# Both mix weights loaded and copied on GpSimd's queue, values loaded two per period, and transfers of the later stages regrouped, in a fused attention, MLP and top-1 mixture kernel

## The chip, the cores and the metric

The kernel runs on one NeuronCore of a Trainium2 chip. The metric is the device time of one execution in microseconds; the time before is the median of three runs. Besides these there is one profiled execution, with a trace of every instruction.

## The reference

Three stages follow each other on 1792 tokens (4 batches of 448) of width 768 (12 heads of 64). Everything is fp32.

```python
def _attn_ref(q, k, v, w_pre, w_post):
    scores = scale * np.matmul(q, k.transpose(0, 1, 3, 2))
    scores = np.einsum('bhij,hg->bgij', scores, w_pre)      # 12x12 mix of the heads
    attn = softmax(scores)                                   # over the keys
    attn = np.einsum('bhij,hg->bgij', attn, w_post)          # 12x12 mix again
    return np.matmul(attn, v)
...
def _moe_ref(x, w_in, w_out):                                # 768 -> 2048 -> 768
    h = x @ w_in
    g = np.where(h > 0.0, h, np.exp(np.minimum(h, 0.0)) - 1.0)
    return g @ w_out
...
def _moe2_ref(x, w_skip, w_gate, w1, w2):                    # 8 experts, 768 -> 1024 -> 768
    do_compute = x @ w_skip > 0
    logits = x @ w_gate
    e_idx, gate_w = argmax(logits), max(softmax(logits))
    y = gate_w * (relu(x @ w1[e_idx]) @ w2[e_idx])           # row by row
    return where(do_compute, x + y, x)
...
    x = _attn_ref(q, k, v, w_pre, w_post).transpose(0, 2, 1, 3).reshape(1792, 768)
    return _moe2_ref(_moe_ref(x, ...), ...)
```

## The kernel before

**Precision.** TensorE multiplies in fp32r. Most operands are split into a high part (a cast on ScalarE) and a low part (a subtraction on VectorE), and each product is made of three matmuls: high by high, low by high, high by low. So each loaded tile passes through two engines before TensorE can use it.

**Attention.** q is handled in tiles of at most 120 queries, k in six pairs of heads per batch. `qk` makes scores and writes them to `s`. `relayout` copies `s` by DMAs on SyncE's queue to tiles `d` (eight, whose first 32 rows are zeroed once by GpSimd memsets, L185), in which queries and heads share the partitions, so that the 12x12 mix becomes a matmul with a matrix that is built once from w_pre (`kpre_low`, `kpre_up`, in `mix_pre`). Softmax follows, then the second mix (`mix_post`, matmul `f`, with `kr`, which is `kposts` scaled by the row sums on GpSimd), then the product with v (`av`). The work runs in periods n: period n mixes units n, ends unit n-1 and computes the scores of a later tile. `load_mix` broadcasts w_pre and w_post, 10 rows of copies each (`pre`, `post`); `kron` spreads each to a block matrix by a VectorE copy and two GpSimd selects; `kposts` then gets three more copies by DMA (L381). All loads and stores of this stage go out on SyncE's queue, in the order of the code. Six values (`v`, one per pair of heads) are loaded at the start of period 0; for the other batches the list `values` is filled as the last tile of a batch is done, two at a time.

**MLP.** Weights come as fp64 bit pieces and are narrowed on the chip to fp32 and partly kept in DRAM (`wf`). `products(s)` makes h (L626), `elu` stores the activations to `gT` in DRAM. `tables()` loads `wgt` (gate and skip weights), turns it by 12 small matmuls, and writes it out as `wg`, which is read back later by a broadcast as `wrow`.

**MLP's second product and routing.** Main loop over 14 token tiles of 128 rows, L899. The last weight pieces are loaded singly by L845 into `raw0`'s two-piece buffers, three in all, split into `w`, and used by tile 0. `load_g(i)` loads tile i's activations `gr` in four pieces. `score` multiplies the finished rows by `wrow` on VectorE; `route` and `seat` give each row a slot with its expert; the two `place_old` calls put rows into the first expert tile while the last are being scored.

**Experts.** `use()` hands out weight parts, each 128x1536, split by ScalarE (`whi`) and VectorE (`wlo`). `gather` fetches an expert's rows `xg` by an indirect DMA from GpSimd's queue; TensorE turns them (`pt`, L1082), and they are split to `xt`. `expert_first` and `expert_second` are an expert's two products. From the fourth expert on the order of experts is decided on the chip: `plan()` computes `swap`, and `reorder()` applies it to the row lists `ids` and gives `ordered`, which the gather of expert 3 and later ones needs.

The order on each engine is the order of the code. What an engine does next waits for semaphores, and nothing behind it on the same engine goes ahead.

Of the kernel before, what the change touches and what calls it, by code (L numbers as in the profile page):

```python
# [8 lines left out]
FP32 = mybir.dt.float32  # L9
# [4 lines left out]
ALU = mybir.AluOpType  # L14
# [64 lines left out]
def attention(tc, q, k, v, w_pre, w_post, xT, mix):  # L79
# [12 lines left out]
    with ExitStack() as ctx, ExitStack() as mixing, ExitStack() as scoring:  # L92
# [90 lines left out]
        n_d = [0]  # L183
        for t in d_all:
            nc.gpsimd.memset(t[:32], 0.0)  # L185

# [129 lines left out]
        def load_mix(w, name):  # L316
            rep = const.tile([BR * H, H], FP32, name=name)
            nc.sync.dma_start(out=rep, in_=w.unsqueeze(0).to_broadcast([BR, H, H]))
            return rep
# [20 lines left out]


        for u in range(3):
            load_q(0, [(2 * u, 2 * u + 2)])
            for p in (2 * u, 2 * u + 1):
                load_k(0, p)
                if p >= 4:
                    break
            if u == 0:
                pre, post = load_mix(w_pre, "pre"), load_mix(w_post, "post")
            if u == 2:  # L350
                split_q(0, 0)
                split_k(0, 0, nc.vector)
                load_k(0, 5)
# [3 lines left out]
        for p in range(NK):  # L357
# [8 lines left out]
            if p == 2:  # L366
# [13 lines left out]
                for z, first in ((1, UP), (0, GAP), (0, UP + GAP)):  # L380
                    nc.sync.dma_start(out=kposts[z][first:first + HP, :], in_=kposts[1][:HP, :])  # L381
        moves.pop()()
# [10 lines left out]
        for n in range(NP):  # L393
# [10 lines left out]
            late = n >= NP - 5  # L404
            while values:
                load_v(*values.pop(0))
            if T2 < len(tiles):
# [68 lines left out]
def mixtures(tc, order, xT, w_in, w_out, w_skip, w_gate, w1, w2, ident, gT, wf, wg, x2d, slots, out):  # L476
# [5 lines left out]
    with ExitStack() as top:  # L482
# [27 lines left out]
        with ExitStack() as ctx:  # L510
# [63 lines left out]
            def tables():  # L574
# [7 lines left out]
                nc.sync.dma_start(out=x2d[NT:NT + 1, :], in_=wgs[0:1, :])  # L582
                nc.sync.dma_start(out=wgt[:, :, :E], in_=w_gate.rearrange("(k p) e -> p k e", p=128))
                nc.sync.dma_start(out=wgt[:, :, E], in_=w_skip.rearrange("(k p) -> p k", p=128))
                nc.sync.dma_start(out=wg[E:E + 1, :], in_=w_skip.unsqueeze(0))
# [125 lines left out]
            elu(1)  # L711
            load_x(3)
            products(2)
            w_jobs(0)
# [30 lines left out]
        with ExitStack() as ctx:  # L745
# [47 lines left out]
            def route(i, lg):  # L793
                mx = st_p.tile([128, 8], FP32, tag="mx", name="mx")
                nc.vector.max(out=mx, in_=lg[:, :E])
                ix = st_p.tile([128, 8], U32, tag="ix", name="ix")
                nc.vector.max_index(out=ix, in_max=mx, in_values=lg[:, :E])
                nmx = st_p.tile([128, 1], FP32, tag="nmx", name="nmx")
                nc.vector.tensor_scalar(out=nmx, in0=mx[:, 0:1], scalar1=-1.0, scalar2=None, op0=ALU.mult)
                ex = st_p.tile([128, E], FP32, tag="ex", name="ex")  # L800
                sm = st_p.tile([128, 1], FP32, tag="sm", name="sm")
                nc.scalar.activation(out=ex, in_=lg[:, :E], func=ACTF.Exp, bias=nmx, accum_out=sm)
                nc.vector.tensor_scalar(out=sm, in0=sm, scalar1=1e-9, scalar2=None, op0=ALU.add)
                nc.vector.reciprocal(out=pairs[:, i, 1:2].bitcast(FP32), in_=sm)
                ef = st_p.tile([128, 1], FP32, tag="ef", name="ef")
                nc.vector.tensor_copy(out=ef, in_=ix[:, 0:1])
                do = st_p.tile([128, 1], FP32, tag="do", name="do")
                nc.vector.tensor_scalar(out=do, in0=lg[:, E:E + 1], scalar1=0.0, scalar2=None, op0=ALU.is_gt)
                oh = st_p.tile([128, E], FP32, tag="oh", name="oh")
                nc.vector.tensor_scalar(out=oh, in0=iota8, scalar1=ef, scalar2=do, op0=ALU.is_equal, op1=ALU.mult)  # L810
                return i, oh, do
# [30 lines left out]
            gs = {0: load_g(0)}  # L842
            for fc in range(EARLY, NF):
                raw = raw0.tile([128, 2 * DM], FP32, tag="w", name="wr")[:, :DM]
                last_wr = nc.sync.dma_start(out=raw, in_=wf[fc - EARLY])  # L845
                wo[fc] = split(raw, ring_a if fc < RA + RB else ring2)
            for part in (slice(0, 5), slice(5, E + 1)):
# [40 lines left out]
            for i, n, fc, cs in work:  # L888
# [35 lines left out]
                if fc == NF - 1:  # L924
                    if 0 in cs:
                        x2 = rows[i] = x2_p.tile([128, DM], FP32, tag="x2", name="x2")
                    for c in cs:
                        to, at = x2[:, cols[c]], po[c][:, :cols[c].stop - cols[c].start]
                        nc.scalar.copy(out=to, in_=at)  # L929
                        if last and c == 1:  # L930
                            turned, freed = score_turned(x2, c)
                            place_old(range(2))
                            logits(turned)
                            place_old(range(2, 5))
                    if 1 in cs:
# [3 lines left out]
            hot = seat(*route(NTILE - 1, lg))  # L939
            place_old(range(5, NK))  # L940
            xt0 = [gh_p.tile([128, 2, GC, 128], FP32R, tag="gh", name=f"xt0{c}") for c in range(2)]
# [8 lines left out]
        with ExitStack() as ctx:  # L950
# [288 lines left out]
            h, ht = new_h(), []  # L1239
            expert_first([0], [h], jobs(((3, 2), turn_h, h, ht, 0)))  # L1240
            expert_second(0, ht, jobs(((0,), turn_h, h, ht, 1), ((2,), turn_x, 1)))
            h = new_h()
            expert_first([1], [h], jobs(((1, 2), turn_x, 2)))
            reorder()
            xg[3] = gather(ids[3])
            base = nc.values_load(tab[0:1, 3, E:E + 1], engines=(SP,), min_val=0, max_val=E * CAP)
# [110 lines left out]
```

## Time and profile before

| what | value |
|---|---|
| median of 3 runs | 1022.62 us (1020.44 to 1026.99) |
| profiled execution, its own time | 1024.68 us |
| its span in the trace | 1022.9 us |
| mean granted clock of TensorE | 0.988 |
| TensorE busy | 982.5 us, 96% |
| VectorE, ScalarE, GpSimd busy | 71%, 54%, 22% |

1.8 us of the profiled time lie outside the span. TensorE is busy for all but 40.4 us of the span, so the table says that a reader has to look for the places where TensorE does nothing, and at what it waits for there.

### The profile page before, as it was taken

The numbers are of one execution on the slowest core, as the hardware profiler recorded it, in microseconds if no ns is written. First come the engines' busy times: TensorE is split into PE (matmuls) and PEld (weight loads), VectorE is DVE, ScalarE is ACT, GpSimd is POOL, SyncE is SP. The second block draws the span as 40 slices with busy tenths as digits, with TensorE's granted clock in tenths as the row PEclk, the third lists the DMA queues.
The fourth block names the chain that finished last, engine by engine and source line by source line (L and its number), as shares of the span: only waits on it lengthen the run. The fifth ranks groups of instructions, "written<-read, shape, count | busy, mean of one in ns | idle before, by whom it ended". The sixth has DMA issues, their size and how long they took to land. (4 is left out here: it accounts for less than half of the span.)

```text
span 1022.9 us, 30007 instructions
## 1 busy us (share of the span) xinstructions
PE 982.5 (96%) x12226; PEld 860.5 (84%) x12226; DVE 725.8 (71%) x1458; ACT 555.9 (54%) x1121; POOL 226.8 (22%) x295
## 2 busy tenths in 40 slices
PE   7899999999998899999999999999999999899997
PEld 4577777777766788999999999999999988799987
DVE  5677776777765777666666477777777748999963
ACT  5687787788765654445444462222222116788851
POOL 2233224224223312232332200010101003321002
PEclk9999999999998989999999999999999999999999
DMA  4665665675646565454665489543434396999800
GB/s 157 214 206 158 218 208 149 205 235 131 216 167 204 160 220 166 156 183 151 227 220 192 140 281 301 155 124 93 123 95 123 99 344 237 393 396 398 322 9 34
DMA packets 132297, 199.67 MB, mean 195 GB/s; under 512 B 35476, under 2 KB 99480, under 8 KB 131901
## 3 DMA queue, kind: packets, MB, share of 16 engines
q1 hardware_dynamic: 130013, 191.27, 56.4%
q0 software_dynamic: 2144, 6.46, 1.6%
q8 instruction: 97, 1.59, 0.7%
q14 instruction: 43, 0.35, 0.1%
HBM read 122.47 MB, written 37.65 MB: 157 GB/s over the span
## 5 line engine op out<-in xcount | busy, mean ns | idle before, releaser
L899 PE MATMUL o<-w,gh 128*128 128x384 f32 (+2 forms) x1344 | 239.2, 337 | 1.2 <-DVE w L505 0.8
L899 PEld LDWEIGHTS o<-w,gh 128*128 128x128 f32 x1344 | 231.9, 188 | 4.5 <-DVE w L505 1.4
L626 PE MATMUL h<-xh,w 128*128 128x448 f32 x1152 | 235.4, 367 | 0.0
L626 PEld LDWEIGHTS h<-xh,w 128*128 128x128 f32 x1152 | 217.4, 189 | 17.3 <-issue 0.4
L265 PEld LDWEIGHTS f<-kr,e 64*64 64x64 f32 x5888 | 106.3, 136 | 39.1 <-issue 29.5
L213 DVE TENSOR_REDUCE nmx<-c 128x1 f32<-128x448 f32 x184 | 102.4, 617 | 51.7 <-PE c L205 51.6
L226 ACT ACTIVATE e<-c,nmx 128x448 f32<-128x448 f32 x184 | 114.2, 632 | 23.0 <-DVE nmx L213 22.8
L789 DVE SCALAR_TENSOR_TENSOR junk<-x,wrow 128x768 f32<-128x768 f32 x117 | 111.8, 955 | 18.3 <-ACT x L929 12.8
L246 POOL TENSOR_SCALAR kr<-kpost,rs 128x60 f32<-128x60 f32 x184 | 78.4, 448 | 200.1 <-DVE rs L241 110.2
L1067 DVE TENSOR_TENSOR wlo<-w1t,whi 128x1536 fp32r<-128x1536 f32 x64 | 111.0, 1751 | 14.3 <-ACT whi L1065 14.0
L265 PE MATMUL f<-kr,e 64*64 64x60 f32 (+1 forms) x5888 | 108.4, 219 | 7.3 <-issue 3.5
L541 POOL TENSOR_TENSOR wf<-a,p 128x768 f32<-128x768 f32 x32 | 66.6, 2081 | 187.2 <-DVE p L539 139.5
L1065 ACT CAST whi<-w1t 128x1536 fp32r<-128x1536 f32 x64 | 93.9, 1482 | 20.6 <-PE ph L1094 9.4
L164 PE MATMUL qk<-k,qq 64*120 64x448 f32 (+1 forms) x576 | 82.6, 408 | 8.1 <-ACT k L135 4.5
L774 ACT CAST gh<-gr 128x512 fp32r<-128x512 f32 x56 | 35.0, 624 | 98.7 <-PE o L899 39.1
L205 PE MATMUL c<-d,kpre_low 64*64 64x448 f32 x368 | 83.3, 554 | 3.0 <-ACT s L168 2.8
L205 PE MATMUL c<-d,kpre_up 60*64 60x448 f32 x368 | 81.8, 554 | 0.0
L271 ACT COPY at<-f 128x420 f32<-128x420 f32 (+1 forms) x136 | 65.4, 516 | 28.2 <-PE f L265 27.2
L164 PEld LDWEIGHTS qk<-k,qq 64*120 64x120 f32 (+1 forms) x576 | 52.1, 186 | 27.8 <-issue 4.6
L286 PE MATMUL xp<-at,v 128*64 128x120 f32 (+1 forms) x1152 | 67.5, 266 | 7.3 <-issue 3.9
L168 ACT ACTIVATE s<-qk 120x448 f32<-120x448 f32 (+1 forms) x96 | 51.7, 544 | 35.5 <-PE qk L164 26.4
L169 DVE TENSOR_SCALAR s<-qk 120x448 f32<-120x448 f32 (+1 forms) x96 | 58.3, 621 | 16.1 <-PE qk L164 8.4
(180 smaller groups left out, 1255.7 us busy)
## 6 DMA issues: line engine op xcount, KB each, us to landing
w1t<-in_moe_w_dram SPq DMA_DIRECT2D x64, 768.0 KB
d<-s SPq DMA_DIRECT2D x176, 210.0 KB
gT<-g SPq DMA_DIRECT2D x64, 224.0 KB
f<-in_moe_w_in_dram SPq DMA_DIRECT2D x16, 768.0 KB
f<-in_moe_w_out_dram SPq DMA_DIRECT2D x16, 768.0 KB
gr<-gT SPq DMA_DIRECT2D x48, 256.0 KB
rk<-in_k_dram SPq DMA_DIRECT2D x24, 224.0 KB
v<-in_v_dram SPq DMA_DIRECT2D x24, 224.0 KB
```

What stands on the lines that cost most here:

```text
L164: nc.tensor.matmul(out=ps[:n, :S], lhsT=qt[T, p // 2][rows, a, p % 2, :n], rhs=kt[b, p][rows, z, :], start=(i == 0), stop=(i == 2))
L205: nc.tensor.matmul(out=ps[j * UP:(j + 1) * UP, :S], lhsT=kpre_up[UP:UP + HP, :] if z else kpre_low, rhs=d[z, j])
L213: nc.vector.tensor_reduce(out=t, in_=c, op=ALU.max, axis=AX.X, negate=True)
L226: nc.scalar.activation(out=e, in_=c, func=ACTF.Exp, bias=t, accum_out=sms[0][:, k + i:k + i + 1])
L246: nc.gpsimd.tensor_scalar(out=kr, in0=kposts[z], scalar1=rs[:, 2 * i + z:2 * i + z + 1], scalar2=None, op0=ALU.mult)
L265: nc.tensor.matmul(out=ps[to, heads, z, :], lhsT=e[rows, keys * JW:(keys + 1) * JW], rhs=kr[rows, first * HR:(first + n) * HR])
L286: nc.tensor.matmul(out=ps[i][z * 64:(z + 1) * 64, :n], lhsT=vt[b, p][:, jc * 2 + z, :], rhs=att[T][:, jc * H + ORDER.index(2 * p + z), :n] ...
L626: nc.tensor.matmul(out=ps, lhsT=w[:, a, kk, :], rhs=xs[tb, kk][:, z, :], start=(kk == 0 and a + z == 0), stop=(kk == NK - 1 and a == 1))
L789: nc.vector.scalar_tensor_tensor(out=t[:, o:o + n], in0=x2, scalar=1.0, in1=w, op0=ALU.mult, op1=ALU.mult, accum_out=lg[:, e:e + 1])
L899: mm = nc.tensor.matmul(out=po[c][:, :cols[c].stop - cols[c].start], lhsT=gs[i][fc // GC][:, a, fc % GC, :], rhs=wo[fc][:, z, cols[c]], st ...
L1065: nc.scalar.copy(out=hi, in_=t)
L1067: nc.vector.tensor_tensor(out=lo, in0=t, in1=hi, op=ALU.subtract)
```

## The change

Seven edits stand in the diff. `pre` and `post` are loaded on GpSimd's queue, ahead of the eight memsets of `d`, and the three copies to `kposts` go out there too. Values are loaded from period 1 on, two per period. The two loads of `wgt` move from `tables()` to a place behind `load_x(3)`, ahead of `products(2)`. The last weight pieces of the MLP are loaded two to a buffer, so that six are under way at once instead of three. `route` computes `oh` ahead of the exponential. One of the pieces of `place_old` moves behind the last `route`. `reorder()` and the gather of expert 3 move ahead of the second product of expert 0.

```diff
-        for t in d_all:
-            nc.gpsimd.memset(t[:32], 0.0)
...
         def load_mix(w, name):
             rep = const.tile([BR * H, H], FP32, name=name)
-            nc.sync.dma_start(out=rep, in_=w.unsqueeze(0).to_broadcast([BR, H, H]))
+            nc.gpsimd.dma_start(out=rep, in_=w.unsqueeze(0).to_broadcast([BR, H, H]))
             return rep
...
+        pre, post = load_mix(w_pre, "pre"), load_mix(w_post, "post")
+        for t in d_all:
+            nc.gpsimd.memset(t[:32], 0.0)
         for u in range(3):
             load_q(0, [(2 * u, 2 * u + 2)])
             for p in (2 * u, 2 * u + 1):
                 load_k(0, p)
                 if p >= 4:
                     break
-            if u == 0:
-                pre, post = load_mix(w_pre, "pre"), load_mix(w_post, "post")
...
                 for z, first in ((1, UP), (0, GAP), (0, UP + GAP)):
-                    nc.sync.dma_start(out=kposts[z][first:first + HP, :], in_=kposts[1][:HP, :])
+                    nc.gpsimd.dma_start(out=kposts[z][first:first + HP, :], in_=kposts[1][:HP, :])
...
-            while values:
-                load_v(*values.pop(0))
+            for bp in values[:2] if n else ():
+                load_v(*bp)
+            del values[:2 if n else 0]
...
-                nc.sync.dma_start(out=wgt[:, :, :E], in_=w_gate.rearrange("(k p) e -> p k e", p=128))
-                nc.sync.dma_start(out=wgt[:, :, E], in_=w_skip.rearrange("(k p) -> p k", p=128))
                 nc.sync.dma_start(out=wg[E:E + 1, :], in_=w_skip.unsqueeze(0))
...
             elu(1)
             load_x(3)
+            nc.sync.dma_start(out=wgt[:, :, :E], in_=w_gate.rearrange("(k p) e -> p k e", p=128))
+            nc.sync.dma_start(out=wgt[:, :, E], in_=w_skip.rearrange("(k p) -> p k", p=128))
             products(2)
...
             gs = {0: load_g(0)}
-            for fc in range(EARLY, NF):
-                raw = raw0.tile([128, 2 * DM], FP32, tag="w", name="wr")[:, :DM]
-                last_wr = nc.sync.dma_start(out=raw, in_=wf[fc - EARLY])
-                wo[fc] = split(raw, ring_a if fc < RA + RB else ring2)
+            for f0 in range(EARLY, NF, 2):
+                raw = raw0.tile([128, 2, DM], FP32, tag="w", name="wr")
+                fcs = range(f0, min(f0 + 2, NF))
+                for fc in fcs:
+                    last_wr = nc.sync.dma_start(out=raw[:, fc - f0], in_=wf[fc - EARLY])
+                for fc in fcs:
+                    wo[fc] = split(raw[:, fc - f0], ring_a if fc < RA + RB else ring2)
...
-                            place_old(range(2, 5))
+                            place_old(range(2, 4))
...
             hot = seat(*route(NTILE - 1, lg))
-            place_old(range(5, NK))
+            place_old(range(4, NK))
...
             expert_first([0], [h], jobs(((3, 2), turn_h, h, ht, 0)))
+            reorder()
+            xg[3] = gather(ids[3])
             expert_second(0, ht, jobs(((0,), turn_h, h, ht, 1), ((2,), turn_x, 1)))
             h = new_h()
             expert_first([1], [h], jobs(((1, 2), turn_x, 2)))
-            reorder()
-            xg[3] = gather(ids[3])
```

In `route` the four operations that make `ef`, `do` and `oh` now stand ahead of those that make `nmx`, `ex` and `sm`; each of them is the same as before.

The first place is SyncE's queue at the change from the first score tile to the first period. Each row is a DMA that the engine issues, with the line, the destination, the source and its size; `d_154` to `d_157` are the last four copies of the first score tile. Before:

```order
L197 DMA d_161<-s 120x1x448
L129 DMA v<-in_v_dram 128x448 x6
L197 DMA d_154<-s 120x1x448
L197 DMA d_155<-s 120x1x448
L197 DMA d_156<-s 120x1x448
L197 DMA d_157<-s 120x1x448
L197 DMA d_158<-s 120x1x448
```

And in the changed kernel:

```order
L195 DMA d_161<-s 120x1x448
L195 DMA d_154<-s 120x1x448
L195 DMA d_155<-s 120x1x448
L195 DMA d_156<-s 120x1x448
L195 DMA d_157<-s 120x1x448
L129 DMA v<-in_v_dram 128x448 x2
L195 DMA d_158<-s 120x1x448
```

The six loads of values stood ahead of the four copies; two of them stand behind now, and the other four in the two periods after that.

The second place is SyncE's queue at the start of the MLP's second product: `wr` are the last weight pieces, `gr` activations of the coming tiles, `wrow` the broadcast gate weights. Before:

```order
L845 DMA wr<-wf_79 128x768
L771 DMA gr<-gT_0_61 128x4x128
L771 DMA gr<-gT_0_65 128x4x128
L637 DMA gT_3_76<-g 128x448
L771 DMA gr<-gT_0_69 128x4x128
L845 DMA wr<-wf_80 128x768
L771 DMA gr<-gT_0_73 128x4x128
L771 DMA gr<-gT_0_61 128x4x128
L845 DMA wr<-wf_81 128x768
L845 DMA wr<-wf_82 128x768
L845 DMA wr<-wf_83 128x768
L849 DMA wrow<-wg 128x3840
```

And in the changed kernel:

```order
L847 DMA wr<-wf_79 128x768
L847 DMA wr<-wf_80 128x768
L635 DMA gT_3_76<-g 128x448
L847 DMA wr<-wf_81 128x768
L847 DMA wr<-wf_82 128x768
L771 DMA gr<-gT_0_61 128x4x128
L771 DMA gr<-gT_0_65 128x4x128
L847 DMA wr<-wf_83 128x768
L852 DMA wrow<-wg 128x3840
L852 DMA wrow<-wg 128x3072
L771 DMA gr<-gT_0_69 128x4x128
L771 DMA gr<-gT_0_73 128x4x128
```

The weight pieces stand together and ahead of the activations, and the last two activations of tile 1 stand behind both halves of `wrow`.

The third place is VectorE in the first expert: `wlo` are weight parts, `ht` turned hidden rows, `swapped` the work of `reorder()`, and the small rows are those of `plan()`. Before:

```order
L976 CAST pair<-ix 128x1
L995 TENSOR_SCALAR ni<-ni 1x8
L1067 TENSOR_TENSOR wlo<-w1t,whi 128x1536
L978 TENSOR_SCALAR pbase<-pair 128x1
L997 TENSOR_SCALAR ov<-ni 1x8
L1084 TENSOR_TENSOR ht_12859<-pt_12860,ht_12859 128x512
L980 TENSOR_SCALAR star<-ebase,pbase 128x8
L989 TENSOR_SCALAR tab<-pbase 1x1
L1067 TENSOR_TENSOR wlo<-w1t,whi 128x1536
```

And in the changed kernel:

```order
L979 CAST pair<-ix 128x1
L998 TENSOR_SCALAR ni<-ni 1x8
L1034 TENSOR_TENSOR swapped<-ids 128x8
L981 TENSOR_SCALAR pbase<-pair 128x1
L1000 TENSOR_SCALAR ov<-ni 1x8
L1070 TENSOR_TENSOR wlo<-w1t,whi 128x1536
L983 TENSOR_SCALAR star<-ebase,pbase 128x8
L992 TENSOR_SCALAR tab<-pbase 1x1
L1087 TENSOR_TENSOR ht_12856<-pt_12857,ht_12856 128x512
L984 TENSOR_SCALAR swap<-star 128x8
L988 TENSOR_TENSOR last<-last,star 1x8
L1001 TENSOR_TENSOR ov<-ov,star 1x8
```

The first operation of `reorder()` that reads `ids` now stands ahead of a weight part. The next weight part stood three rows behind the first `ht`; now 13 rows lie between them, four of them operations of `reorder()`, one the second `ht`, the others those of `plan()`.

## Rows read from the trace of the kernel before

**Rows 1.** Waits of TensorE over the whole span: us in total, times, longest.

```profile
PE pt L1082 <- DMA xg<-x2d,ordered: 3.0, 1, 3.0
...
PE c L205 <- ACT s L168: 2.8, 1, 2.8
PE pt L589 <- DMA wgt<-in_moe_w_gate_dram: 2.2, 1, 2.2
...
PE o L899 <- DVE w L505: 0.8, 2, 0.4
...
PE o L899 <- ACT w L504: 0.4, 2, 0.2
```

**Rows 2.** Timeline 0 to 24: start, us, engine, line, operation [idle before <-releaser].

```profile
1.55 3.35 POOL L185 MEMSET d<- 32x448 f32 x8
2.18 1.03 SPq L318 DMA_DIRECT2D pre<-in_w_pre_dram  x1
...
3.31 0.41 DVE L147 TENSOR_TENSOR qq<-rq,qq 128x240 fp32r<-128x240 f32 x1 [2.25 <-ACT qq L142]
...
4.09 0.48 SPq L119 DMA_DIRECT2D rq<-in_q_dram  x1
...
6.34 0.39 ACT L142 CAST qq<-rq 128x240 fp32r<-128x240 f32 x1 [1.28 <-DMA rq<-in_q_dram]
...
10.11 0.21 DVE L329 COPY kpre_kr<-pre 120x120 f32<-120x120 f32 x1
```

**Rows 3.** Timeline 24 to 50: SyncE's issues, and the engines that follow.

```profile
24.24 3.13 SPq L129 DMA_DIRECT2D v<-in_v_dram  x6
...
26.39 1.66 POOL L246 TENSOR_SCALAR kr<-kpost,rs 128x60 f32<-128x60 f32 x4 [14.48 <-DVE rs L241]
...
27.47 7.00 SPq L197 DMA_DIRECT2D d<-s  x8
...
35.39 0.98 ACT L168 ACTIVATE s<-qk 120x448 f32<-120x448 f32 x2 [3.82 <-DMA d<-s]
```

**Rows 4.** SyncE's queue, 355 to 425: the load of `wgt`.

```profile
398.37 0.40 SPq L583 DMA_DIRECT2D wgt<-in_moe_w_gate_dram  x1
```

**Rows 5.** Timeline 585 to 640: last weight pieces, gate broadcast, TensorE, scoring.

```profile
605.87 2.66 SPq L845 DMA_DIRECT2D wr<-wf  x3
...
608.63 0.85 SPq L849 DMA_DIRECT2D wrow<-wg  x2
...
614.63 17.67 PE L899 MATMUL o<-w,gh 128*128 128x384 f32 x100 [0.38 <-DVE w L505]
...
617.55 0.96 DVE L789 SCALAR_TENSOR_TENSOR junk<-x,wrow 128x768 f32<-128x768 f32 x1 [2.98 <-DMA wrow<-wg]
```

**Rows 6.** Timelines 822 to 862 and 862 to 905: row lists, weight parts, gather.

```profile
851.95 0.91 POOL L1190 DMA_DIRECT2D ids<-slots  x1
...
857.28 0.13 DVE L976 CAST pair<-ix 128x1 f32<-128x1 uint32 x1
...
860.26 1.73 DVE L1067 TENSOR_TENSOR wlo<-w1t,whi 128x1536 fp32r<-128x1536 f32 x1
...
863.60 0.71 PEld L1107 LDWEIGHTS y<-wlo,ht 128*128 128x128 f32 x4
...
881.48 2.25 POOL L1072 DMA_INDIRECT xg<-x2d,ordered  x1 [6.36 <-DVE ordered L1035]
...
889.73 0.30 PE L1082 MATMUL pt<-ident,xg 128*128 128x128 f32 x1 [3.02 <-DMA xg<-x2d,ordered]
```

**Rows 7.** DMA issues 848 to 862, 875 to 892; last the us to landing.

```profile
ids<-slots POOLq DMA_DIRECT2D x1, 5.0 KB, 4.7
...
xg<-x2d,ordered POOLq DMA_INDIRECT x3, 7.1
out_dram<-y,ids POOLq DMA_INDIRECT x1, 9.3
```

**Rows 8.** Stretch 860 to 880: PE, PEld, DVE, ACT, POOL busy; clock, DMA, GB/s.

```profile
860.00:880.00 20.00, 20.00 (x106) 17.84 (x105) 20.00 (x42) 15.54 (x17) 3.84 (x1) 1.00 1.04 395
```

More of the change, by code (lines that the diff above doesn't have):

```diff
@@ L797, in route @@
                 nc.vector.max_index(out=ix, in_max=mx, in_values=lg[:, :E])
+                ef = st_p.tile([128, 1], FP32, tag="ef", name="ef")
+                nc.vector.tensor_copy(out=ef, in_=ix[:, 0:1])
+                do = st_p.tile([128, 1], FP32, tag="do", name="do")
+                nc.vector.tensor_scalar(out=do, in0=lg[:, E:E + 1], scalar1=0.0, scalar2=None, op0=ALU.is_gt)
+                oh = st_p.tile([128, E], FP32, tag="oh", name="oh")
+                nc.vector.tensor_scalar(out=oh, in0=iota8, scalar1=ef, scalar2=do, op0=ALU.is_equal, op1=ALU.mult)
                 nmx = st_p.tile([128, 1], FP32, tag="nmx", name="nmx")
@@ L804, in route @@
                 nc.vector.reciprocal(out=pairs[:, i, 1:2].bitcast(FP32), in_=sm)
[L805 to L810, printed above, removed]
                 return i, oh, do
```

## The prediction

> **What bounds the kernel now.** The table of the profile comes first: TensorE is busy for 982.5 of 1022.9 us, the next engine for 71%. So the work itself can't be shortened by this change, which takes away no matmul, and the sum is made over TensorE's gaps. The second view is TensorE's list of waits. Four of its entries lie in places that the diff touches [rows 1]: 3.0 us for the gathered rows `xg`, 2.8 us for ScalarE's score copy `s`, 2.2 us for `wgt`, and 0.8 and 0.4 us for the weight halves `w`. Together that is 9.2 us. The third view, the timeline around each gap, says what was late there, and what comes next if it is on time. The first 13 us are a case apart: TensorE waits for ScalarE and VectorE, which wait for the first loads.
>
> **The start.** SyncE issues `pre` from 2.18 and `post` behind it, and only then, at 4.09, the second part of q [rows 2]. Without the two that issue could stand at 2.18, so 1.91 us earlier. What it is worth is read from the reader: ScalarE stood idle for 1.28 us before the cast at 6.34 that needs it [rows 2]. The cast would follow the engine's earlier casts at once, and the chain behind it (k casts, VectorE's k low, TensorE's scores) is one long row of work that moves with it. I take 1.3 us; 1.9 is the upper end, should the loads of k behind it also come sooner.
> On GpSimd's queue the two stand ahead of the memsets, so their issue begins near 1.55. The trace has no plain broadcast on that queue. The nearest rows are the 5 KB of `ids`, 4.7 us to landing, and a store of 9.3 us, the slowest of that queue there [rows 7]. Landing lies between 6.3 and 11.4 then. They are needed where VectorE copies `pre`, at 10.11 before, so at 8.8 now. The `ids` row is nearest in size (5.6 KB here), so I take nothing; at the far end VectorE waits 2.6 us and the start loses 1.3 instead of gaining it. The memsets slip by about two issues, and the first write to `d` comes only after a whole tile's scores. The three copies to `kposts` move to a queue that is idle for 14.48 us before `kr` reads them at 26.39 [rows 3]; their cost is nothing, and what SyncE saves there was covered by its wait for `s`.
>
> **The values.** Six loads take SyncE's queue from 24.24 to 27.37, ahead of the last four `d` copies of the first score tile. These start at 27.47, and ScalarE waits 3.82 us, to 35.39, until they have read `s` [rows 3]. TensorE's 2.8 us hang on that wait. Without the six ahead the copies start some 3.1 us sooner, and 1.34 MB of transfers with them don't lie ahead. ScalarE's wait falls from 3.82 to 0.7 at most, and to nothing if the transfers gain too. TensorE's 2.84 goes wholly or nearly so: I take 2.8, with 2.0 as the lower end. What takes over is the exponentials, which fill ScalarE there. The values are first read in the fifth period, by the code (`n >= 4`), and the last two are asked for in the fourth; the reads then wait only if a 224 KB load takes a whole period. The later batches were filled two at a time before, so nothing changes for them.
>
> **The gate weights.** `wgt` is asked for at 398.37 [rows 4], and TensorE waits for it 2.2 us [rows 1]. Moved ahead of `products(2)`, the load has some 25 us. It puts about 1 us of issue on SyncE ahead of later loads with slack. The 12 small matmuls now stand behind 126 products instead of 175, and their copies lie beside TensorE's next products. I take 2.2, all of it.
>
> **The weight pieces.** TensorE waits 0.8 and 0.4 us [rows 1], since the last three pieces are issued only from 605.87, when buffers come free [rows 5]. Six under way at once remove these: 1.2 us. The price lies in the queue: two activation loads of tile 1 now stand behind both halves of `wrow`. Three pieces and the first half of `wrow`, 3.1 MB, came between 605.87 and 617.55 [rows 5], so at 269 GB/s or more. The second half and one activation load, 1.8 MB, follow at 269 to 395 GB/s [rows 5, 8], that is 4.6 to 6.8 us. `wrow` is issued some 4 us sooner than at 608.63, its first half lands near 613.6, and the first of the two loads at 618.2 to 620.4. TensorE comes to it halfway through tile 1, near 622.7 by the 0.177 us per matmul of [rows 5], and casts and VectorE's scoring want it some 1 to 1.5 us before. The margin is 1 to 3 us. I take 0.9, with 1.2 and -1 as ends.
> The trace shows `wrow` landing behind everything issued before it on SyncE's queue. The Trainium skill says in "DMA: Bandwidth & Descriptors", "Queues, rings and completion order", that each DMA engine consumes one issuer's descriptors in ring order, so the activations can't overtake the 3.5 MB; by a free overtaking the sum would have 1.2 here instead of 0.9.
>
> **The route.** `oh` ahead of the exponential lets the slots be written sooner by four small operations, about 0.5 us; TensorE is busy at that place with `place_old`. Nothing.
>
> **The reorder.** The gather for expert 3 is issued at 881.48 and takes 7.1 us; TensorE waits 3.02 until 889.73 [rows 6, 7], so it wants the rows at 886.7. From its new place the gather goes out near 865 and lands by about 873. The 3.0 go away, but VectorE pays: it is busy for 20.00 of the 20 us from 860 [rows 8], and seven small operations, an estimate of 0.1 us each from the 0.13 of `pair` [rows 6], now lie ahead of weight parts. The part written from 860.26 to 861.99 is needed at 863.60 [rows 6]; it slips by about 1.6 and lands on that edge. I charge 0.6 us and take 2.4. The ends are 3.0 and 0: the first operation of `reorder()` now follows `pair` at 857.28, and `ids`, issued at 851.95, lands 4.7 us after that, at 856.65 or, from the issue's end, 857.6. At 9.3 us VectorE would stand still for 4 us, and TensorE's stall at 863.60 would be as large as the gain.
>
> **The sum.** 1.3 + 2.8 + 2.2 + 0.9 + 0 + 2.4 = 9.6 us. The profiled execution took 1024.68, which makes 1015.1. It lies 2.06 above the median; against the median of 1022.62 the forecast is 1013.0, or 0.94% less. A measurement of this kernel tells about 1%, 10.2 us, from no change, so the sum lies just short of that.
>
> **The rivals.**
> *All gaps close in full.* 1.9 + 2.84 + 2.2 + 1.2 + 3.0 = 11.1, so 1011.5, and 1010.5 if the earlier slots give 1 us. For it: each of the named releasers moves by several us, more than its wait. Against it: 20.00 busy [rows 8].
> *VectorE gives the gather's gain back.* `ids` late or the weight parts late, as above: the last term 0 to -0.5, the sum 6.7 to 7.2, so 1015.4 to 1015.9. For it: no slack at 857.28 and 863.60 [rows 6].
> *Activations behind `wrow` stall tile 1.* The fourth term falls from 0.9 to -1: sum 7.7, so 1014.9.
> *The gap at 33 us stays.* The change doesn't do what it says if SyncE's own issues, 7.00 us for 8 copies [rows 3], were the bound, or the slower chain of ScalarE. Then the second term is 0: sum 6.8, 1015.8.
> *Slower: the broadcasts come late.* VectorE takes its work in order; its copy of `pre` stands ahead of k low, on which TensorE's scores hang. Past 8.8 us each microsecond of lateness is paid in full by the whole kernel. It is slower than before if `post` lands after 8.8 + 9.6 = 18.4 us, 17 us from its issue; at 20 it gives 1024.2. Against it: no DMA of that queue in those stretches needs over 9.3 [rows 7]. VectorE stood idle for 2.25 us before 3.31 [rows 2], so it keeps nothing from GpSimd while these two are issued. The Trainium skill ("SBUF — State Buffer", "SBUF: two separate sides") has a rule that speaks against the queue: while VectorE runs certain copies in its two-port mode, GpSimd can't write the descriptors of its own DMAs. By that rule these two go out freely, and the three of `kposts` may be held for some copies of below 1 us each, which nobody feels before 26.39.
>
> **How the numbers follow.** The forecast, between 1011.8 and 1014.6, gets 0.55; full closing 0.13; VectorE giving back 0.14; tile 1's stall 0.07; the gap at 33 us 0.07; slower 0.04. Two of the smaller losses at once give about 1018. The range from 1010.5 to 1018.5 leaves out the slow rival and some of what the median of a few runs scatters by (1020.44 to 1026.99 before). Faster by over 1% means below 1012.4: full closing, and about two fifths of the forecast's chance, since that bound lies 0.6 below its middle: 0.36. Slower by over 1%: half of its rival, and a little for scatter, 0.03. Within 1%: 0.61.
>
> **What the changed kernel's profile would show.** TensorE's list of waits without the entries for `xg` by `ordered`, `wgt` and `s` at L168, and those of `w` below 0.3; ScalarE's second q cast at about 5.1, VectorE's `pre` copy at about 8.8 without a wait for a DMA; the gather near 865; no wait of TensorE for `gh` at 622 or `wlo` at 863 above 1 us. The prediction is wrong if TensorE's busy time changes (its clock, or contention), if the start doesn't move at all, or if a new wait of over 2 us stands at one of those places.

## The result and the profile after

| kernel | median, us | runs | ratio to the kernel before, 95% interval |
|---|---|---|---|
| before | 1026.25 (1020.22 to 1030.22) | 9 | |
| changed | 1011.38 (1009.51 to 1017.13) | 9 | 0.9873 (0.9842 to 0.9904) |

The change makes the kernel 1.27% faster, between 0.96 and 1.58%. Of 1026.25 us that is 13.0 us, 9.8 at the lower end. The forecast was 9.6 us (0.94%, just below that lower end), and 1013.0 for the time. The measured 1011.38 lies in the stated range, 0.4 us below the stretch that was given to the forecast itself and next to the rival of full closing (1011.5).

The profiled execution of the changed kernel took 1012.51 us, 12.2 less than the one before. Its page, busy time of each engine:

```profile
PE 979.1 (97%) x12226; PEld 859.0 (85%) x12226; DVE 724.3 (72%) x1458; ACT 556.3 (55%) x1121; POOL 247.9 (25%) x300
```

TensorE's busy time is 3.4 us shorter than before, its idle time 31.7 instead of 40.4 us. The busy time follows the clock: TensorE's granted clock was 0.83 from 290 to 300 us and 0.69 from 355 to 366 us in the execution before, 1.00 and 0.84 in this one, which at half speed makes 3.4 us, in places where the change has no part. TensorE's list of waits in the changed kernel, from its top:

```profile
PE qk L164 <- ACT k L135: 4.7, 1, 4.7
PE xp L284 <- issue: 3.6, 4, 1.9
PE f L263 <- DVE at L269: 3.3, 1, 3.3
PE xp L284 <- DVE x L300: 2.9, 1, 2.9
PE f L263 <- issue: 2.2, 4, 1.0
PE f L263 <- ACT at L269: 1.5, 3, 0.5
```

The entries for `xg` by `ordered`, `c` by `s`, `wgt` and `w` [rows 1] are all gone. What heads the list now stood there before, in places that the change doesn't touch. So the gaps are closed; how much each was worth, the list doesn't say. For that I set the end of the same matmul in both traces side by side (each counted from the first of its line's tile) and looked at how far it moved across each place:

| place in the program | forecast, us | moved in the changed kernel | moved with this part alone |
|---|---|---|---|
| start, to 26 us | -1.3 | +0.2 | +0.1 |
| values, 26 to 47 us | -2.8 | -3.6 | -3.6 |
| `wgt`, 386 to 410 us | -2.2 | -2.5 | -2.5 |
| weight pieces, 608 to 617 us | -0.9 | -2.2 | -2.2 |
| route, 836 to 858 us | 0 | -0.1 | not run alone |
| reorder, 886 to 895 us | -2.4 | -3.2 | -3.2 |
| sum | -9.6 | -11.4 | |

From 47 to 386 us, where the change has no part, the changed kernel's execution moved by another 1.0 us, so that all comes to 12.4.

**The start**, timeline 0 to 13 of the changed kernel (columns as in [rows 2]):

```profile
1.65 0.83 POOL L316 DMA_DIRECT2D pre<-in_w_pre_dram  x1
2.17 0.43 SPq L119 DMA_DIRECT2D rq<-in_q_dram  x1
...
6.77 0.39 ACT L142 CAST qq<-rq 128x240 fp32r<-128x240 f32 x1 [1.56 <-DMA rq<-in_q_dram]
...
10.02 0.21 DVE L327 COPY kpre_kr<-pre 120x120 f32<-120x120 f32 x1
```

The second q load is issued 1.92 us sooner than before, as forecast, but its cast comes 0.43 us later: 4.6 us from issue to cast, where it was 2.25 [rows 2]. The trace's DMA packets, told apart by their sizes (960 bytes for q, 1792 for k), say more: before, this load's packets begin 1.1 us after its issue and are through in 0.8 us; in the changed kernel the first begins only at 4.05, as the k loads issued ahead of it end, and they spread over 2.2 us among those of the next k load and of the broadcasts. The copy of `pre` waits for nothing.

**The values**, timeline 24 to 50:

```profile
23.28 4.36 SPq L195 DMA_DIRECT2D d<-s  x5
...
27.69 1.39 SPq L129 DMA_DIRECT2D v<-in_v_dram  x2
...
29.26 3.42 SPq L195 DMA_DIRECT2D d<-s  x4
...
31.61 1.03 ACT L168 ACTIVATE s<-qk 120x448 f32<-120x448 f32 x2
```

The copies go out ahead of the values, and ScalarE's `s`, which waited 3.82 us [rows 3], starts 3.8 us sooner without any wait.

**`wgt`**, SyncE's queue, then TensorE in the timeline 375 to 400:

```profile
368.54 0.43 SPq L711 DMA_DIRECT2D wgt<-in_moe_w_gate_dram  x1
```

```profile
385.07 0.82 PE L587 MATMUL pt<-ident,wgt 128*8 128x128 f32 x6
```

16.5 us lie between issue and use, and TensorE doesn't wait.

**The weight pieces**, timeline 580 to 632:

```profile
589.56 33.59 PE L902 MATMUL o<-w,gh 128*128 128x384 f32 x192
...
598.94 0.86 SPq L852 DMA_DIRECT2D wrow<-wg  x2
...
608.20 0.96 DVE L789 SCALAR_TENSOR_TENSOR junk<-x,wrow 128x768 f32<-128x768 f32 x1 [4.16 <-DMA wrow<-wg]
...
612.92 1.35 ACT L774 CAST gh<-gr 128x512 fp32r<-128x512 f32 x2 [5.75 <-DMA gr<-gT]
```

192 matmuls run without a break through both tiles. The two activations behind `wrow` come late, as the rival had it: ScalarE waits 5.75 us for them. At 0.175 us per matmul (33.59 / 192) and 96 matmuls per tile, tile 1 needs them near 614.8, half a tile behind tile 0's end at 606.4. The high halves are done from 613.6 on. It is just enough.

**The reorder**, timeline 840 to 866:

```profile
842.12 0.91 POOL L1193 DMA_DIRECT2D ids<-slots  x1
...
848.16 0.15 DVE L1034 TENSOR_TENSOR swapped<-ids 128x8 int32<-128x8 int32 x1
...
851.74 0.95 POOL L1075 DMA_INDIRECT xg<-x2d,ordered  x1 [2.81 <-DVE swapped L1039]
...
852.35 1.74 DVE L1070 TENSOR_TENSOR wlo<-w1t,whi 128x1536 fp32r<-128x1536 f32 x1
...
854.41 0.71 PEld L1110 LDWEIGHTS y<-wlo,ht 128*128 128x128 f32 x4
```

The gather goes out 29.7 us sooner than before (881.48, [rows 6]). VectorE's first read of `ids` stands right behind `pair`, without a wait. The weight part ends at 854.09, and the weight load that needs it follows at 854.41: the edge that the prediction spoke of, with 0.3 us to spare.

### The profile page after: what moved, and what is told of

It reads as the page before. It is cut to its first block, busy times and chain, and to the rows that moved or that the text cites. A ratio compares the mean times of both kernels' runs of the same rounds, so it can differ in the third digit from the quotient of the medians.

```text
span 1010.8 us, 30008 instructions
## 1 busy us (share of the span) xinstructions
PE 979.1 (97%) x12226; PEld 859.0 (85%) x12226; DVE 724.3 (72%) x1458; ACT 556.3 (55%) x1121; POOL 247.9 (25%) x300
## 5 line engine op out<-in xcount | busy, mean ns | idle before, releaser
L837 POOL DMA_INDIRECT slots<-pairs,si x14 | 18.8, 1346 | 204.4 <-DVE si L836 155.8
```

## The experiments

Of each of the first four kernels there is one execution, with its profile; ratios stand only for the eight that follow.

### The start alone

The kernel before, with these lines of the change and no others; the memsets stand behind the broadcasts.

```diff
-            nc.sync.dma_start(out=rep, in_=w.unsqueeze(0).to_broadcast([BR, H, H]))
+            nc.gpsimd.dma_start(out=rep, in_=w.unsqueeze(0).to_broadcast([BR, H, H]))
...
+        pre, post = load_mix(w_pre, "pre"), load_mix(w_post, "post")
+        for t in d_all:
+            nc.gpsimd.memset(t[:32], 0.0)
...
-                    nc.sync.dma_start(out=kposts[z][first:first + HP, :], in_=kposts[1][:HP, :])
+                    nc.gpsimd.dma_start(out=kposts[z][first:first + HP, :], in_=kposts[1][:HP, :])
```

> The kernel before with the start alone: both broadcasts and the copies to kposts on GpSimd's queue, nothing else. In the changed kernel the second part of q was issued 1.92 us sooner (2.17 instead of 4.09) and cast 0.43 us later (6.77 instead of 6.34). First theory: the broadcasts' transfers on GpSimd's queue hold up the loads beside them. Second theory: the loads are bound by their bytes, whoever else transfers. Both expect of this run what the changed kernel showed: second q cast at 6.3 to 6.9, TensorE's scores at 15 us within 0.3 us of their old place, the six loads of values still ahead of the copies and TensorE's gap of 2.8 us near 33 still there. Third theory (it was chance of one execution): the cast at about 5.1 and all of TensorE's work from 10 us on some 1.2 us earlier.

Timeline 0 to 13 of this kernel:

```profile
2.17 0.43 SPq L119 DMA_DIRECT2D rq<-in_q_dram  x1
...
6.74 0.39 ACT L142 CAST qq<-rq 128x240 fp32r<-128x240 f32 x1 [1.64 <-DMA rq<-in_q_dram]
```

The same late load again, TensorE within 0.2 us of its old place at 15 and at 25 us, and the gap near 33 still there, 3.1 us. So it isn't chance.

### Both broadcasts on SyncE's queue, behind the first loads

On the changed kernel:

```diff
-            nc.gpsimd.dma_start(out=rep, in_=w.unsqueeze(0).to_broadcast([BR, H, H]))
+            nc.sync.dma_start(out=rep, in_=w.unsqueeze(0).to_broadcast([BR, H, H]))
...
-        pre, post = load_mix(w_pre, "pre"), load_mix(w_post, "post")
...
                 load_k(0, 5)
+                pre, post = load_mix(w_pre, "pre"), load_mix(w_post, "post")
```

> The changed kernel with both broadcasts on SyncE's queue, behind the first tile's q and k loads, instead of GpSimd's. First theory (GpSimd's transfers hold up the loads): the second q cast comes at 5.2 to 5.6 instead of 6.77, and TensorE's scores follow about 1 us earlier than in the changed kernel, unless VectorE then waits for pre (needed at about 9). Second theory (bytes): the cast stays at 6.3 to 6.8 and the scores stay within 0.3 us.

```profile
2.18 0.43 SPq L119 DMA_DIRECT2D rq<-in_q_dram  x1
...
6.15 0.39 ACT L142 CAST qq<-rq 128x240 fp32r<-128x240 f32 x1 [1.03 <-DMA rq<-in_q_dram]
```

Half of what the first theory said: the cast comes 0.6 us sooner than in the changed kernel, not 1.2 to 1.6. TensorE's scores at 15 us stand 0.5 sooner. A second execution of this kernel has the cast at 6.42. SyncE's issues stand where they stood, so this is what GpSimd's broadcasts cost the load. The transfer rates don't carry it. Stretch 4 to 6 us in the changed kernel, in a second execution of it, then in this one (last columns: TensorE's granted clock, DMA share, GB/s):

```profile
4.00:6.00 2.00, 1.32 (x6) 0.87 (x8) 1.20 (x2) 1.13 (x2) 2.00 (x6) 1.00 0.64 157
```

```profile
4.00:6.00 2.00, 1.49 (x6) 1.06 (x8) 1.25 (x2) 1.02 (x2) 2.00 (x7) 1.00 0.85 222
```

```profile
4.00:6.00 2.00, 1.42 (x6) 0.97 (x8) 1.22 (x2) 1.10 (x2) 0.92 (x3) 1.00 0.86 224
```

With GpSimd's two small broadcasts beside them the loads ran at 157 GB/s in one execution and at 222 in the other, and the cast was late in both (6.77 and 6.64). What differs is the load's last packets: they begin at 6.21 and 6.06 with GpSimd's broadcasts (6.06 in the kernel with the start alone too), at 5.36 and 5.77 without.

### Both broadcasts on ScalarE's queue

On the changed kernel:

```diff
-            nc.gpsimd.dma_start(out=rep, in_=w.unsqueeze(0).to_broadcast([BR, H, H]))
+            nc.scalar.dma_start(out=rep, in_=w.unsqueeze(0).to_broadcast([BR, H, H]))
```

> The changed kernel with both broadcasts issued on ScalarE's queue at the very start instead of GpSimd's, beside the same loads. First theory, that it is GpSimd's queue that holds up the loads: second q cast at 5.2 to 5.6. Rival within it, that any broadcast of 240 rows of 48 bytes beside the loads holds them up: the cast at 6.3 to 6.9 as in the changed kernel. Second theory (bytes): 6.3 to 6.9 too. ScalarE's own issues, about 0.8 us each, may delay its first casts by up to 1 us, and then the cast by the same.

```profile
5.55 0.39 ACT L142 CAST qq<-rq 128x240 fp32r<-128x240 f32 x1
6.69 0.56 ACT L135 CAST k<-rk 128x448 fp32r<-128x448 f32 x1 [0.75 <-DMA rk<-in_k_dram]
```

Two broadcasts of the same 240 rows of 48 bytes don't hold this load up as GpSimd's do. But how much of that is the queue stays open here, since SyncE's next issues are later too: the third q load goes out at 4.63, where it was 3.60. Here the cast of q comes at 5.55 and waits for nothing, though ScalarE's own issues made its first casts late. But now the next thing is late: the k load, cast at 6.69. TensorE's scores at 15 us again stand only 0.6 us sooner than in the changed kernel.

### Both broadcasts on GpSimd's queue, behind the memsets

On the changed kernel:

```diff
-        pre, post = load_mix(w_pre, "pre"), load_mix(w_post, "post")
         for t in d_all:
             nc.gpsimd.memset(t[:32], 0.0)
+        pre, post = load_mix(w_pre, "pre"), load_mix(w_post, "post")
```

> The changed kernel with both broadcasts still on GpSimd's queue, but behind the memsets of d, so that their issue begins near 5 instead of 1.65. First theory: the second q load has no such transfer beside it and its cast comes at 5.2 to 5.6; the later loads may be held up instead, and pre lands 4.6 us after its issue, near 9.6, so that VectorE waits 0.5 to 1.5 us for it and the gain is lost there. Second theory: the cast stays at 6.3 to 6.8.

```profile
4.87 0.83 POOL L316 DMA_DIRECT2D pre<-in_w_pre_dram  x1
...
5.95 0.39 ACT L142 CAST qq<-rq 128x240 fp32r<-128x240 f32 x1 [0.85 <-DMA rq<-in_q_dram]
```

The same two transfers, issued when the q load is nearly through, cost it little: cast at 5.95. VectorE waited 0.36 us for `post` and not for `pre`. TensorE gained 0.5 us at 15 us and had lost it again by 25.6 us, behind a wait of 0.80 us for ScalarE's exponentials at 24.05.

### The four other parts, each alone on the kernel before

Each kernel has its piece of the change and nothing else. Values:

```diff
-            while values:
-                load_v(*values.pop(0))
+            for bp in values[:2] if n else ():
+                load_v(*bp)
+            del values[:2 if n else 0]
```

> The kernel before with the values alone: two per period from period 1 on. First theory (each part removes its own gap, and the parts add): TensorE's gap of 2.8 us near 33 is gone, its work from 37 us on lies 2.6 to 3.2 earlier than before, all other gaps stand; 0.25 to 0.35% less in all. Rival (SyncE's issues of the copies, or ScalarE, are the bound there): a gap of over 1 us stays near 33.

Gate weights, out of `tables()`:

```diff
             load_x(3)
+            nc.sync.dma_start(out=wgt[:, :, :E], in_=w_gate.rearrange("(k p) e -> p k e", p=128))
+            nc.sync.dma_start(out=wgt[:, :, E], in_=w_skip.rearrange("(k p) -> p k", p=128))
             products(2)
```

> The kernel before with the loads of wgt alone moved behind the third load of x. First theory: TensorE's 2.2 us for wgt go, its work behind 405 us lies 2.2 to 2.6 earlier than ahead of 385; 0.2 to 0.25% less in all. Rival (the two loads, with rows of 32 bytes and of 4, delay the loads and stores behind them on SyncE's queue): a new wait of TensorE for w_in or x between 380 and 420.

Weight pieces:

```diff
-            for fc in range(EARLY, NF):
-                raw = raw0.tile([128, 2 * DM], FP32, tag="w", name="wr")[:, :DM]
...
+            for f0 in range(EARLY, NF, 2):
+                raw = raw0.tile([128, 2, DM], FP32, tag="w", name="wr")
...
```

> The kernel before with the last weight pieces loaded two to a buffer, nothing else. In the changed kernel TensorE's work moved by 2.24 us here, where the list of waits had 1.2. First theory: a short wait costs TensorE more than its idle time shows, since 14 matmuls took 4.4 us from 610.23 to 614.63 where at 0.177 us each they take 2.5; then TensorE's work behind 617 lies 1.9 to 2.4 earlier than ahead of 608. Rival: 1.2 from here, and the other 1.0 came with another part (the earlier wgt), then 1.0 to 1.4. Other rival (activations behind the gate broadcast): a new wait of TensorE in tile 1.

Reorder, from behind the next expert's first product:

```diff
             expert_first([0], [h], jobs(((3, 2), turn_h, h, ht, 0)))
+            reorder()
+            xg[3] = gather(ids[3])
             expert_second(0, ht, jobs(((0,), turn_h, h, ht, 1), ((2,), turn_x, 1)))
```

> The kernel before with the row lists' reordering and the gather of expert 3 ahead of the first expert's second product, nothing else. Here the slots aren't written sooner, as they are in the changed kernel, where ids were issued 0.6 us sooner against TensorE's work. First theory (the gap goes in full, VectorE has room): 3.0 to 3.3 us from 895 us on and no new wait at 857 to 870. Rival (VectorE waits for ids or its weight parts come late without the earlier slots): new waits of TensorE for weight parts between 858 and 872, 0.3 to 3 us, and a net gain below 2.7.

| part alone | median of 10 runs, us | ratio to the kernel before, 95% interval |
|---|---|---|
| before | 1023.79 | |
| values | 1020.09 | 0.9982 (0.9965 to 0.9999) |
| gate weights | 1019.55 | 0.9960 (0.9932 to 0.9987) |
| weight pieces | 1019.82 | 0.9971 (0.9944 to 0.9998) |
| reorder | 1020.87 | 0.9961 (0.9925 to 0.9996) |

Each interval lies below 1, that of the values by 0.0001. The product of the four ratios is 0.9875, the ratio of the changed kernel 0.9873, as it would be if the parts add and nothing is left over for the start. But the ratios are too wide to size a part by (0.2 to 0.35% each side; by the medians of the table the product would be 0.9856), so the sum alone doesn't show it. The sizes stand in the table of shifts, where each part alone repeats what it did in the changed kernel.

Values: no gap of TensorE near 33. ScalarE's `s` starts at 31.45 without a wait. The rival fell.

Gate weights: no new wait between 380 and 420. The rival fell.

Weight pieces, TensorE from 595 to 625 in this kernel:

```profile
594.72 30.44 PE L902 MATMUL o<-w,gh 128*128 128x384 f32 x174
```

No break, and a shift of 2.2 us as in the changed kernel. So the 1.0 that the list of waits doesn't have belongs to this place and came with no other part. TensorE in the kernel before, 600 to 617:

```profile
599.78 10.45 PE L899 MATMUL o<-w,gh 128*128 128x384 f32 x59
610.47 0.61 PE L899 MATMUL o<-w,gh 128*128 128x384 f32 x2 [0.24 <-ACT w L504]
611.46 2.01 PE L899 MATMUL o<-w,gh 128*128 128x384 f32 x10 [0.38 <-DVE w L505]
613.63 0.61 PE L899 MATMUL o<-w,gh 128*128 128x384 f32 x2 [0.17 <-ACT w L504]
614.63 2.70 PE L899 MATMUL o<-w,gh 128*128 128x384 f32 x14 [0.38 <-DVE w L505]
```

TensorE's work ahead of the first break ends at 610.23 and that behind the last begins at 614.63; the 14 matmuls between took 4.4 us with their waits, and at 0.177 us they are worth 2.5. That makes 1.9 of the 2.2 us, where the waits listed come to 1.17. The first theory holds, both rivals fell.

Reorder, timeline 850 to 870 in this kernel:

```profile
857.08 0.15 DVE L1031 TENSOR_TENSOR swapped<-ids 128x8 int32<-128x8 int32 x1
...
860.66 0.94 POOL L1072 DMA_INDIRECT xg<-x2d,ordered  x1 [2.82 <-DVE swapped L1036]
...
861.27 1.74 DVE L1067 TENSOR_TENSOR wlo<-w1t,whi 128x1536 fp32r<-128x1536 f32 x1
...
863.33 0.71 PEld L1107 LDWEIGHTS y<-wlo,ht 128*128 128x128 f32 x4
```

Without the earlier slots too, `ids` are there in time and the weight part ends at 863.01, 0.3 us ahead of its use. Before, 1.6 us lay between that part's end at 861.99 and its use at 863.60 [rows 6]: 1.3 us of slack are spent, and no more than that. In this execution the rival fell. It came in another one, that of the broadcasts behind the memsets:

```profile
850.90 0.17 DVE L1034 TENSOR_TENSOR swapped<-ids 128x8 int32<-128x8 int32 x1 [1.84 <-DMA ids<-slots]
...
853.70 1.67 PE L1110 MATMUL y<-whi,ht 128*128 128x384 f32 x8 [1.71 <-DVE ht L1087]
```

There `ids`, issued at 843.95, held VectorE up for 1.84 us, TensorE then waited 1.71 us for `ht`, and its work fell back by 2.0 us, more than half of what the earlier gather gave. Of the nine executions with the earlier gather this is the only one with such a stall; VectorE waits 0.16 us in one more.

### The start undone, and two other starts measured

The kernel without the start is the changed one with the lines of the first experiment taken back (below, two of them); the last two kernels are those of the second and third experiment.

```diff
-            nc.gpsimd.dma_start(out=rep, in_=w.unsqueeze(0).to_broadcast([BR, H, H]))
+            nc.sync.dma_start(out=rep, in_=w.unsqueeze(0).to_broadcast([BR, H, H]))
```

> The changed kernel once more, as the base for the three beside it. The four parts alone gave 0.9982, 0.9960, 0.9971 and 0.9961, whose product is 0.9875. First theory (the parts add and the start gives nothing): 0.987 to 0.988. If the parts overlapped, a ratio nearer to 1 than 0.990.

> The changed kernel with its start undone: both broadcasts, the memsets and the copies to kposts where they were, on SyncE's queue. First theory (the start gives nothing in all, since GpSimd's transfers take back what SyncE's issues gave): TensorE's work at 15 us and at 25 us within 0.3 us of the changed kernel's, ratio within 0.002 of it. Rival (the start is worth the predicted 1.3 somewhere later, or SyncE's saved issues of kposts are): 0.13% slower than the changed kernel, and TensorE's work about 1.3 us later from 40 us on.

> The changed kernel with both broadcasts on ScalarE's queue, measured. TensorE's work at 15 us came 0.6 us earlier there than in the changed kernel, and the one execution took 1006.08 us. First theory (executions scatter by several us through the granted clock and pace, and only the 0.6 us is the edit's): ratio 0.0003 to 0.001 below that of the changed kernel, not to be told from it. Rival (the queue is worth more): 0.003 or more below.

> The changed kernel with both broadcasts on SyncE's queue behind the first loads, measured. TensorE's work at 15 us came 0.5 us earlier than in the changed kernel and 0.9 at 45. First theory: ratio 0.0005 to 0.001 below that of the changed kernel, not to be told from it. Rival (it is worth more, or the queue order harms later): 0.003 away, either way.

| kernel | median of 6 runs, us | ratio to the kernel before (1024.99), 95% interval |
|---|---|---|
| changed, again | 1012.78 | 0.9896 (0.9861 to 0.9930) |
| changed, start undone | 1012.93 | 0.9884 (0.9850 to 0.9919) |
| broadcasts on ScalarE's queue | 1011.69 | 0.9876 (0.9842 to 0.9910) |
| broadcasts on SyncE's queue, behind the loads | 1011.67 | 0.9876 (0.9842 to 0.9910) |

The four can't be told apart. The changed kernel's second ratio, 0.9896, lies outside the 0.987 to 0.988 that were expected, and its interval holds both those and values above 0.990. With the start undone TensorE's work from 14 to 55 us lies within 0.4 us of the changed kernel's first execution, mostly on the early side, and by up to 0.75 us on the late side of its second. So no gain of the start shows, and neither other start is shown to be better than the changed kernel. The 1006.08 us of one execution with ScalarE's queue was scatter: six more gave 1006.72 to 1014.69.

## Why the prediction held, and where its terms were off

The time lies in the range and near the forecast, and the way there was right in the main: the sum over TensorE's gaps, four of which closed. Two kinds of error lay in the terms, of opposite sign: the start came out 1.5 us short, and the four gaps, forecast at 8.3, moved TensorE by 11.5. That they partly cancel is luck. So is some of the nearness of the time: the kernel before had a median of 1022.62 us when the forecast was made from it and of 1026.25 beside the changed one.

Of the signs of being wrong that the prediction names, two came: the start didn't move, and TensorE's busy time changed, by the 3.4 us of the clock. The third, a new wait of over 2 us, didn't come in the changed kernel.

**The start: the term of 1.3 is 0.** The step that failed is the sentence "The cast would follow the engine's earlier casts at once". I moved the issue and took the landing to move with it. Three things stood against that. The load had to come behind the k loads issued ahead of it: in each of these kernels its first packet begins at 3.7 to 4.05 us, whoever issued the broadcasts. GpSimd's broadcasts beside it cost some more: 4.5 to 4.6 us from issue to cast in three executions with them, 4.0 and 4.2 with the broadcasts behind the loads on SyncE's queue, 3.8 with GpSimd's issued later. And where q does come sooner, the k load is next, so that TensorE gains 0.2 to 0.7 us at 15 us on the changed kernel's first execution, which a later wait for ScalarE's exponentials can take back by 25 us. Why the load's packets then spread over some 2 us on SyncE's queue without GpSimd's beside them, where they took 0.8 before, no run separates. The bound below, -1.3, wasn't reached either: `pre` landed 4.6 us after its issue, and 3.4 us in the second execution, near the 4.7 of the `ids` row.

**The closed gaps: each worth more than its idle time.** The values moved TensorE by 3.6 us (forecast 2.8, idle 2.84), `wgt` by 2.5 (2.2, idle 2.19), the pieces by 2.2 (0.9, idle 1.17), the reorder by 3.2 (2.4, idle 3.02). Part of this is idle time that the list doesn't count, because a matmul that stands around the gap is shown as busy for longer: the two matmuls that start at 35.98 behind the gap last 0.96 us; in the changed kernel the same two, without a gap, 0.58. The rest of it isn't explained. With four short waits in a row, as at the pieces, the difference is as large as the waits. So "upper end 1.2" was no upper end.

**The deductions that weren't due.** For activations behind `wrow` I took off 0.3. They landed as reckoned: TensorE comes to this stage 6.9 us sooner than before, so the cast at 612.92 is 619.8 in the time of before, and 618.2 to 620.4 was the reckoning. What shrank the margin is TensorE, whose need at 614.8 is 621.7 in that time, since the closed gaps bring it 2.2 us sooner; the 622.7 of the prediction left its own gain out, and is itself 1.1 short (tile 0 ends 4 matmuls behind 614.63, and 52 at 0.177 us make 623.8). The loads still met it. For VectorE's extra work at the reorder I took off 0.6: the weight part slipped 1.3 against TensorE's work, and its slack was 1.6. Both were right about the place, and both had margins of about a microsecond or less in the end; the one at the row lists gave way in one execution of nine.

**The rivals.** Tile 1's stall and the gap that stays at 33 us: neither came, by the rows above. VectorE giving back the gather's gain came in one kernel's execution, with `ids` late as that rival has it, and in neither execution of the changed kernel. The slower one didn't come; in the changed kernel the copy of `pre` waits for no DMA. Of the rule that was weighed there, by the Trainium skill ("SBUF — State Buffer", "SBUF: two separate sides"), that VectorE can keep GpSimd from writing its descriptors, nothing showed: `pre` landed 4.6 us after its issue, from 1.65 with VectorE idle as from 4.87 with VectorE at work; whether that work was in the mode that the rule is about, the trace doesn't tell. That each DMA engine consumes one issuer's descriptors in ring order, as the Trainium skill has it ("DMA: Bandwidth & Descriptors", "Queues, rings and completion order"), agrees with ScalarE's 5.75 us wait for the activations behind `wrow`.

**What isn't the change's.** The same kernel run again gave 0.9896 after 0.9873, and its profiled execution has a span of 1005.7 us against 1010.8. The two executions differ between 120 and 360 us, where the change has nothing. So the 1.0 us that the table of shifts has there needs no cause in the edit; both measurements' intervals hold 11.4 (1.11% of 1024.68).

**What the table of shifts can't see.** It compares with one execution, and what the gaps cost differs between executions. The kernel with the start alone, around the gap near 33 and the one near 885 (columns: us; busy PE, PEld, DVE, ACT, POOL; granted clock, DMA share, GB/s):

```profile
35.00:43.00 8.00, 6.61 (x90) 5.12 (x92) 4.73 (x11) 5.30 (x15) 0.04 (x1) 0.57 0.64 209
883.00:893.00 10.00, 7.31 (x29) 6.99 (x29) 6.66 (x5) 4.63 (x5) 0.57 (x1) 0.66 1.04 393
```

Here TensorE's clock fell to the lower of its two levels (1.2 instead of 2.4 GHz) for 6.8 us at each of the two gaps, and TensorE's work behind them came 1.6 and 2.5 us later than in the one execution of the kernel before, whose clock stayed at 1.00 there. Of five executions with the gap at 33 us three had such a fall, of five with the gap at 885 two; of the nine executions without the one gap, and the nine without the other, none had. Averaged over the five, that adds some 0.5 and 0.7 us to what the two gaps cost, an estimate from few executions. It would bring 11.4 to about 12.6, beside the 13.0 measured.

## What to carry to other kernels

Where one engine is busy for 96%, its list of waits names the places to mend, and here the gains add; but size a gap by how far the work behind it moves against its undisturbed pace (matmuls times the pace), not by the idle column, above all where several short waits follow each other. An issue that moves is no landing that moves: ask what shares the DMA engines in that stretch, and which transfer is late next. And where a moved operation lands on the edge of its slack, an estimate of half a microsecond off is as likely too much as too little: look for the reader's first use and subtract, in more than one execution: the edge that held in eight gave way in the ninth.

## What the runs showed of the hardware that was not expected

Two broadcasts of 5.6 KB each on GpSimd's queue, issued beside loads on SyncE's queue, made a load of 120 KB there take 4.5 to 4.6 us from issue to cast in three executions; with the same two behind the loads on SyncE's queue it took 4.0 and 4.2.

A gap of 2.6 to 3.1 us in TensorE's work, at 33 or at 885 us, came with 3.4 or 6.8 us at the lower clock in five cases of ten; the fall lies between 1.0 us ahead of the gap's end and 1.5 us behind it.

In two of the profiled executions TensorE kept a slower pace over a whole stage, without any wait and at a granted clock of 1.00. The matmuls `h` in the stretch 430 to 580, in the kernel before and then in the one with the values alone (columns: count, busy us, mean ns, idle):

```profile
L626 PE MATMUL h<-xh,w 128*128 128x448 f32 x744 | 150.6, 365 | 0.0
```

```profile
L627 PE MATMUL h<-xh,w 128*128 128x448 f32 x728 | 150.5, 368 | 0.0
```

150 us hold 16 matmuls fewer, 2.2%; from 420 to 606 us TensorE's work fell back by 3.7 us. The kernel with the reorder alone had the same (x728). What sets it, no run here tells.
